# A mixture of experts behind retention: blocks of up to 768 tokens, weights loaded in slices by ScalarE, tokens transposed between products

## Chip, cores and metric

One Trainium2 chip, one core. The metric is the device time of one execution in microseconds (us). The engines are TensorE (PE; its weight loads are PEld), VectorE (DVE), ScalarE (ACT), GpSimd (POOL) and SyncE (SP). Each has its own instruction stream, and all share 16 DMA engines.

## What is computed

Retention for 8 sequences of 576 tokens with 8 heads, and then a mixture of 8 experts in which a token takes the expert of the token before it or its own best one. Every token has exactly one expert. Cut to what matters here:

```python
for b in range(B):                       # 8 x 576 tokens, D = 512
    for s in range(S):
        fresh_e = int(np.argmax(logits[b, s]))
        e = fresh_e if s == 0 or local_gate[b, s] < 0.5 else prev_e
        ...
        h = np.maximum(x[b, s] @ w1[e], 0.0)      # 512 -> 1024
        out[b, s] = p[e] * (h @ w2[e])            # 1024 -> 512
```

All of it is float32. w1 and w2 of one expert are 2 MB each.

## The kernel before, in words

**First stage** (lines 82 to 406). Retention and routing run over 36 chunks of 128 tokens. The rows x go to a DRAM buffer `xd`; `route` scatters each token's number and gate value into a DRAM table `slots` sorted by expert (L323, GpSimd, 36 scatters, each ordered behind the one before). At its end VectorE cuts each expert's tokens into blocks and writes a table `desc`: for block j the arm of the Switch, the expert, the first row, and whether it is used. The cut (L346 to L349) takes blocks of FULL = 256 tokens and leaves a last one of up to TMAX = 512.

**Expert stage** (lines 409 to 507). `step(j)` reads the arm's number for block j on every engine (L485) and jumps into one of 10 bodies, one for each width in SIZES (multiples of 32 from 256 up), or into a last one that finishes the work (L492). 17 steps are unrolled. An arm does this:

- `load(j + 1)`: SP loads the rows of `slots` (L433), GpSimd gathers the tokens into `xg` 128 at a time (L435, four gathers), SP loads the next block's w1 and w2, four transfers of 512 KB each (L444). w1 has two buffers, w2 three.
- `block(j, T)`: TensorE transposes each group of 128 tokens (L468, four transposes into one of two PSUM buffers `xgps`). A copy takes it to `xT`: even groups by VectorE (L470), odd ones by ScalarE (L472).
- TensorE then runs group 0 of the block before, which was held back for this place: `group(j - 1, 0)`, eight products 128x128 by 128x512 (L453), scaled by VectorE (L456) and scattered to `out` by GpSimd (L457).
- The first layer: for each of 8 slices m, four products of width T into `hps` (L478, three PSUM buffers), and a ReLU on ScalarE into `hT` (L480).
- The second layer for groups 1 and up of this block (L453).

A float32 product shows as two MATMUL instructions in the trace: 16 for a group of the second layer, 64 for the first layer of a block. The scheduler of the tile framework may move independent instructions inside an arm, but not across the Switch.

Of the kernel before, what the change touches and what calls it, by code (L numbers as in the profile page):

```python
# [9 lines left out]
F32 = mybir.dt.float32  # L10
BF16 = mybir.dt.bfloat16
I32 = mybir.dt.int32
Act = mybir.ActivationFunctionType
Alu = mybir.AluOpType
AX = mybir.AxisListType
ET = mybir.EngineType
# [3 lines left out]
P = 128  # L20
B, H, S, DH = 8, 8, 576, 64
D = H * DH
E, F = 8, 1024
DK, FK = D // P, F // P
# [7 lines left out]

CAP = NTOK
Q = 4
FULL = 256
TMAX = 512
GMAX = TMAX // P

NBLK = E + 1 + (NTOK - E - TMAX) // FULL
NSURE = 2 * E + 1  # L40

SIZES = [0, P, FULL] + list(range(FULL + 32, TMAX + 1, 32))
NOWHERE = 2 * NTOK
GW = 32

# [2 lines left out]
def kernel(  # L48
# [10 lines left out]
    nc = tc.nc  # L59

    def pool(stack, name, bufs, space=None):
        kw = {} if space is None else {"space": space}
        return stack.enter_context(tc.tile_pool(name=name, bufs=bufs, **kw))
# [3 lines left out]
    w1s = [keep.tile([P, FK, DK, P], F32, name="w1s0")]  # L67
    w2s = [keep.tile([P, FK, D], F32, name="w2s0")]
# [5 lines left out]
    desc = keep.tile([1, 4, NBLK + 1], I32, name="desc")  # L74
    make_identity(nc, ident)

    xgs = [keep.tile([P, GMAX, D], F32, name=f"xg{i}") for i in range(2)]
    for t in xgs:
# [3 lines left out]
    with ExitStack() as part:  # L82
# [23 lines left out]
        for k in range(DK):  # L106
# [5 lines left out]
            out=mask, in_=mask, compare_op=Alu.is_ge, fill=0.0,  # L112
# [8 lines left out]
        def number(name, shape, pattern, base=0, channel=0, dtype=F32):  # L121
# [11 lines left out]
        before = once.tile([P, P], BF16, name="before")  # L133
        nc.gpsimd.memset(before, 1.0)
        nc.gpsimd.affine_select(
            out=before, in_=before, compare_op=Alu.is_gt, fill=0.0,
# [17 lines left out]
                            in_=empty.rearrange("p r t -> p (r t)"))  # L154
# [187 lines left out]
        n = rt.tile([P, E], F32, name="n")  # L342
        nc.vector.tensor_tensor(n, base, base0, op=Alu.subtract)
        nb = rt.tile([P, E], F32, name="nb")
        nbi = rt.tile([P, E], I32, name="nbi")
        nc.vector.tensor_scalar(nb, n, -1.0, None, Alu.add)  # L346
        nc.vector.tensor_copy(nbi, nb)
        nc.vector.tensor_scalar(nbi, nbi, FULL.bit_length() - 1, None, Alu.arith_shift_right)
        nc.vector.tensor_copy(nb, nbi)  # L349
# [28 lines left out]
        nc.vector.tensor_tensor(at, one_of_blk, its_first, op=Alu.subtract)  # L378
        nc.vector.tensor_scalar(at, at, float(FULL), None, Alu.mult)
        nc.vector.tensor_tensor(its_n, its_n, at, op=Alu.subtract)  # L380
        more = rt.tile([P, (NBLK + 1)], F32, name="more")
        nc.vector.tensor_scalar(more, its_n, float(TMAX), None, Alu.is_gt)
        over = rt.tile([P, (NBLK + 1)], F32, name="over")
        nc.vector.tensor_scalar(over, its_n, -float(FULL), None, Alu.add)
        nc.vector.tensor_tensor(over, over, more, op=Alu.mult)
        sizes = rt.tile([P, (NBLK + 1)], F32, name="sizes")
        nc.vector.tensor_tensor(sizes, its_n, over, op=Alu.subtract)
        used = rt.tile([P, NBLK + 1], F32, name="used")
        nc.vector.tensor_scalar(used, sizes, 0.0, None, Alu.is_gt)
        kind = rt.tile([P, NBLK + 1], F32, name="kind")  # L390
        nc.vector.tensor_copy(kind, used)
        for t in SIZES[1:-1]:
            nc.vector.scalar_tensor_tensor(kind, sizes, float(t), kind, Alu.is_gt, Alu.add)

        ends = rt.tile([P, NBLK + 1], F32, name="ends")
        nc.vector.tensor_tensor(ends[:, 1:], used[:, 0:NBLK], used[:, 1:], op=Alu.subtract)
        nc.vector.scalar_tensor_tensor(kind[:, 1:], ends[:, 1:], float(len(SIZES)), kind[:, 1:],
                                       Alu.mult, Alu.add)
# [4 lines left out]
        nc.vector.scalar_tensor_tensor(at, its_e, float(CAP), at, Alu.mult, Alu.add)  # L403
        nc.vector.tensor_scalar(more, sizes, 0.0, float(E * CAP - TMAX), Alu.is_le, Alu.mult)
        nc.vector.tensor_tensor(at, at, more, op=Alu.max)
# [1 line left out]


    io = pool(ctx, "io", 2)
    mid = pool(ctx, "mid", 2)  # L410
    ps_x = pool(ctx, "ps_x", 2, PSUM)
    ps_h = pool(ctx, "ps_h", 3, PSUM)
    ps_y = pool(ctx, "ps_y", 3, PSUM)
    CUT = 4

    later = pool(ctx, "later", 1)
    w1s += [later.tile([P, FK, DK, P], F32, name="w1s1")]
    w2s += [later.tile([P, FK, D], F32, name=f"w2s{i}") for i in range(1, 3)]  # L420
    hTs = [later.tile([P, FK, TMAX], F32, name=f"hT{i}") for i in range(2)]
    slot_of = [later.tile([P, GMAX, 2], I32, name=f"slot{i}") for i in range(3)]

    def load(j):

        slot = slot_of[j % 3]
        e = nc.values_load(desc[0:1, 1, j:j + 1], engines=[ET.SP], min_val=0, max_val=E - 1,
                           skip_runtime_bounds_check_because="a count of experts before it")
        at = nc.values_load(desc[0:1, 2, j:j + 1], engines=[ET.SP], min_val=0, max_val=E * CAP - TMAX,
                            skip_runtime_bounds_check_because="the blocks end where the rows do")  # L430
        used = nc.values_load(desc[0:1, 3, j:j + 1], engines=[ET.SP], min_val=0, max_val=1,
                              skip_runtime_bounds_check_because="a comparison")
        nc.sync.dma_start(out=slot, in_=slots[bass.ds(at, TMAX), :].rearrange("(g p) t -> p g t", p=P))  # L433
        for g in range(GMAX):
            nc.gpsimd.indirect_dma_start(  # L435
                out=xgs[j % 2][:, g, :], out_offset=None, in_=xd,
                in_offset=bass.IndirectOffsetOnAxis(ap=slot[:, g, 0:1], axis=0),
                bounds_check=NTOK - 1, oob_is_err=False)
        f = FK // CUT
        for t, src in ((w1s[j % 2].rearrange("p m k f -> p (m k f)"), w1),  # L440
                       (w2s[j % 3].rearrange("p m d -> p (m d)"), w2)):
            for i in range(CUT):
                cols = slice(i * f * D, (i + 1) * f * D)
                nc.sync.dma_start(out=t[:, cols],  # L444
                                  in_=src[bass.ds(e, 1)].rearrange("o p x -> (o p) x")[:, cols],
                                  cond=used > 0)

    def group(j, g, M):

        hT, slot, w = hTs[j % 2], slot_of[j % 3], w2s[j % 3]  # L450
        yps = ps_y.tile([P, D], F32, name="yps")
        for m in range(FK):
            nc.tensor.matmul(yps[0:M], lhsT=hT[:, m, g * P:g * P + M], rhs=w[:, m, :],  # L453
                             start=(m == 0), stop=(m == FK - 1))
        y = io.tile([P, D], F32, name="y", bufs=4)
        nc.vector.tensor_scalar(y[0:M], yps[0:M], slot.bitcast(F32)[0:M, g, 1:2], None, Alu.mult)  # L456
        nc.gpsimd.indirect_dma_start(  # L457
            out=out, out_offset=bass.IndirectOffsetOnAxis(ap=slot[0:M, g, 0:1], axis=0),
            in_=y[0:M], in_offset=None, bounds_check=NTOK - 1, oob_is_err=False)

    def block(j, T):
        xg = xgs[j % 2]
        groups = [(g, min(P, T - g * P)) for g in range(-(-T // P))]
        xT = mid.tile([P, DK, TMAX], F32, name="xTs")
        for g, M in groups:
            xps = ps_x.tile([P, DK, P], F32, name="xgps")
            for c in range(DK):
                nc.tensor.transpose(xps[:, c, 0:M], xg[0:M, g, c * P:(c + 1) * P], ident[0:M, 0:M])  # L468
            if g % 2 == 0:
                nc.vector.tensor_copy(xT[:, :, g * P:g * P + M], xps[:, :, 0:M])  # L470
            else:
                nc.scalar.copy(xT[:, :, g * P:g * P + M], xps[:, :, 0:M])  # L472
        if j:
            group(j - 1, 0, P)
        for m in range(FK):
            hps = ps_h.tile([P, TMAX], F32, name="hps")
            for c in range(DK):
                nc.tensor.matmul(hps[:, 0:T], lhsT=w1s[j % 2][:, m, c, :], rhs=xT[:, c, 0:T],  # L478
                                 start=(c == 0), stop=(c == DK - 1))
            nc.scalar.activation(hTs[j % 2][:, m, 0:T], hps[:, 0:T], Act.Relu)  # L480
        for g, M in groups[1:]:
            group(j, g, M)

# [1 line left out]
        return nc.values_load(desc[0:1, 0, j:j + 1], min_val=0, max_val=len(SIZES),  # L485
                              skip_runtime_bounds_check_because="a count of sizes")

    load(0)

    def step(j):  # L490
        kind = kind_of(j)
        for k in tc.Switch(kind, len(SIZES) + 1):  # L492
            if k == len(SIZES):
                if j:
                    group(j - 1, 0, P)
            elif SIZES[k] and j < NBLK:
                load(j + 1)
                block(j, SIZES[k])

    for j in range(NSURE):  # L500
        step(j)

    more = nc.values_load(desc[0:1, 3, NSURE - 1:NSURE], min_val=0, max_val=1,
                          skip_runtime_bounds_check_because="a comparison")
    with tc.If(more > 0):
        for j in range(NSURE, NBLK + 1):
            step(j)
# [54 lines left out]
```

## Time and profile before

| | us |
|---|---|
| median of three runs | 992.52 (991.65 to 996.45) |
| the profiled execution: its time | 998.53 |
| its span, first to last instruction | 996.8 |
| PE busy in the span | 792.8 (80%) |
| DVE, ACT, POOL busy | 183.5, 116.9, 191.1 |
| mean granted TensorE clock, of 2.4 GHz | 0.906 |
| one fill of an `xg` buffer at the start (L79, POOL) | 1.80 |
| one copy of a transposed group by ScalarE (L472), mean | 0.57 |
| one comparison of the table of widths (L393, DVE; nine of them) | 0.19 |

The trace has lists of instructions in order of time, sums of waits by line, the sequencers' own instructions by line, and windows with the clock and the DMA rate. "Issue" as the cause of a wait means that the engine waited for nothing that the profile shows. In a timeline each row gives start, duration, engine, line, tiles, shape and count; brackets hold the idle time before it and what ended it.

### The profile page before, as it was taken

What the parts mean: (1) busy time and instruction counts of PE and PEld (TensorE: products, weight loads), DVE (VectorE), ACT (ScalarE), POOL (GpSimd) and SP (SyncE); (2) the same over time, 40 slices, a digit from 0 to 9 for tenths busy, and PEclk for the clock granted to TensorE, in tenths of its full rate; (3) what the DMA queues carried; (4) which work ended last, traced back from release to release, by engine and by line L of the source; (5) the groups of instructions that cost most, each with busy time, mean ns of one, the idle gap of its engine ahead of it and who ended that gap; (6) DMA issues with size and microseconds to landing.
All of it is one profiled execution on the core that took longest, in us unless ns stands there. A gap on an engine that the chain in (4) does not pass through costs nothing. (4 is left out here: it accounts for less than half of the span.)

```text
span 996.8 us, 12627 instructions
## 1 busy us (share of the span) xinstructions
PE 792.8 (80%) x4385; PEld 508.5 (51%) x4385; DVE 183.5 (18%) x486; ACT 116.9 (12%) x291; POOL 191.1 (19%) x208
## 2 busy tenths in 40 slices
PE   5999886868046898599959859887985986998793
PEld 5777675746034444363635536364553644546351
DVE  3565562645400001000000000100000010000000
ACT  1222221212001000010101101010110101001010
POOL 4123233222220202020220202022020121202200
PEclk9999897989568899899979979997997999898898
DMA  8787774761087206433360651336065153315000
GB/s 329 257 231 201 206 216 129 201 197 54 3 299 279 76 12 212 122 128 98 135 236 14 214 178 61 127 125 216 15 211 184 56 191 122 151 40 189 23 20 22
DMA packets 49499, 144.11 MB, mean 145 GB/s; under 512 B 16476, under 2 KB 16604, under 8 KB 44512
## 3 DMA queue, kind: packets, MB, share of 16 engines
q1 hardware_dynamic: 37776, 114.38, 34.8%
q0 software_dynamic: 9616, 23.12, 7.2%
q14 instruction: 288, 2.36, 0.8%
q8 instruction: 91, 1.49, 0.8%
q10 hardware_dynamic: 1728, 2.76, 0.7%
HBM read 129.41 MB, written 19.47 MB: 149 GB/s over the span
## 5 line engine op out<-in xcount | busy, mean ns | idle before, releaser
L453 PE MATMUL yps<-w2s,hT 128*128 128x512 f32 (+3 forms) x656 | 303.7, 619 | 1.1 <-DVE y L456 1.1
L478 PE MATMUL hps<-xTs,w1s 128*128 128x256 f32 (+4 forms) x1024 | 266.0, 422 | 23.5 <-issue 22.6
L478 PEld LDWEIGHTS hps<-xTs,w1s 128*128 128x128 f32 x1024 | 199.2, 195 | 94.2 <-issue 41.9
L453 PEld LDWEIGHTS yps<-w2s,hT 128*128 128x128 f32 (+3 forms) x656 | 121.8, 189 | 162.5 <-issue 160.2
L456 DVE TENSOR_SCALAR y<-yps,slot 128x512 f32<-128x512 f32 (+3 forms) x41 | 30.7, 749 | 497.1 <-PE yps L453 470.4
L468 PE MATMUL xgps<-ident,xg 128*128 128x128 f32 (+3 forms) x164 | 25.2, 298 | 115.9 <-DVE xTs L470 80.6
L457 POOL DMA_INDIRECT out_dram<-y,slot x41 | 40.7, 993 | 396.1 <-DVE y L456 382.2
L435 POOL DMA_INDIRECT xg<-xd,slot x68 | 68.8, 1012 | 205.9 <-issue 129.4
L480 ACT ACTIVATE hT<-hps 128x256 f32<-128x256 f32 (+4 forms) x128 | 53.3, 417 | 422.7 <-PE hps L478 358.4
L468 PEld LDWEIGHTS xgps<-ident,xg 128*128 128x128 f32 (+3 forms) x164 | 19.8, 160 | 129.9 <-DVE xTs L470 84.0
L174 PE MATMUL sps<-ld 64*128 64x128 f32 x576 | 52.8, 314 | 31.1 <-DVE sT L178 20.7
L323 POOL DMA_INDIRECT slots<-slot,posi x36 | 37.1, 1030 | 158.2 <-DMA slots<-slot,posi 94.8
L174 PEld LDWEIGHTS sps<-ld 64*128 64x128 f32 x576 | 43.0, 209 | 33.6 <-DVE sT L178 23.2
L178 DVE TENSOR_TENSOR sT<-sps,mask 128x512 f32<-128x512 f32 x72 | 46.5, 683 | 39.9 <-PE sps L174 39.8
L470 DVE COPY xTs<-xgps 128x512 f32<-128x512 f32 (+3 forms) x24 | 14.9, 619 | 176.9 <-issue 83.4
L194 PE MATMUL ops<-sT,vs 128*64 128x128 f32 x576 | 44.9, 303 | 1.8 <-POOL vs L167 1.8
L167 POOL TENSOR_TENSOR vs<-ld,deck 128x512 f32<-128x512 f32 x36 | 37.3, 1046 | 33.1 <-DMA ld<-in_qkv_dram 26.7
L215 ACT COPY state<-kv 64x256 f32<-64x256 f32 x64 | 23.4, 366 | 160.0 <-PE kv L210 159.2
L194 PEld LDWEIGHTS ops<-sT,vs 128*64 128x64 f32 x576 | 35.1, 151 | 7.7 <-issue 2.9
L200 PE MATMUL ops<-ld,state 128*128 128x128 f32 (+1 forms) x256 | 37.9, 292 | 0.0
L472 ACT COPY xTs<-xgps 128x512 f32<-128x512 f32 (+1 forms) x17 | 9.6, 566 | 226.1 <-PE xgps L468 226.1
L200 PEld LDWEIGHTS ops<-ld,state 128*128 128x128 f32 x256 | 31.9, 196 | 5.9 <-issue 5.9
(117 smaller groups left out, 297.8 us busy)
## 6 DMA issues: line engine op xcount, KB each, us to landing
ld<-in_qkv_dram SPq DMA_DIRECT2D x36, 1024.0 KB
w1s<-in_w_dram SPq DMA_DIRECT2D x68, 512.0 KB
w2s<-in_w_dram SPq DMA_DIRECT2D x68, 512.0 KB
xd<-x SPq DMA_DIRECT2D x36, 256.0 KB
decq<-in_dq_dram ACTq DMA_DIRECT2D x9, 256.0 KB
xg<-xd,slot POOLq DMA_INDIRECT x68, 4.4
out_dram<-y,slot POOLq DMA_INDIRECT x41, 2.8
slots<-slot,posi POOLq DMA_INDIRECT x36, 5.7
```

What stands on the lines that cost most here:

```text
L167: nc.gpsimd.tensor_tensor(vs.rearrange("p (h d) -> p h d", h=H), vn.rearrange("p (h d) -> p h d", h=H), deck[:, m, :].unsqueeze(2).to_broa ...
L174: nc.tensor.matmul(sps[u][:, c, :], lhsT=kT[r, c, :], rhs=qT[r, c, :], start=True, stop=True, skip_group_check=True)
L178: nc.vector.tensor_tensor(sT[:, u], sps[u], (mask2 if m == MID else mask).unsqueeze(1).to_broadcast([P, HP, P]), op=Alu.mult)
L194: nc.tensor.matmul(ops[r, c, :], lhsT=vs[:, h * DH:(h + 1) * DH], rhs=sT[:, u, c, :], start=(c == 0), stop=(m == 0), skip_group_check=True)
L200: nc.tensor.matmul(ops[:, c, 0:n], lhsT=states[(i + 1) % 2][:, c, :], rhs=qT[:, c, 0:n], start=False, stop=True, skip_group_check=True)
L323: nc.gpsimd.indirect_dma_start(out=slots, out_offset=bass.IndirectOffsetOnAxis(ap=posi[:, k:k + 1], axis=0), in_=slot[:, k, :], in_offset= ...
L435: nc.gpsimd.indirect_dma_start(out=xgs[j % 2][:, g, :], out_offset=None, in_=xd, in_offset=bass.IndirectOffsetOnAxis(ap=slot[:, g, 0:1], a ...
L453: nc.tensor.matmul(yps[0:M], lhsT=hT[:, m, g * P:g * P + M], rhs=w[:, m, :], start=(m == 0), stop=(m == FK - 1))
L457: nc.gpsimd.indirect_dma_start(out=out, out_offset=bass.IndirectOffsetOnAxis(ap=slot[0:M, g, 0:1], axis=0), in_=y[0:M], in_offset=None, bo ...
L468: nc.tensor.transpose(xps[:, c, 0:M], xg[0:M, g, c * P:(c + 1) * P], ident[0:M, 0:M])
L478: nc.tensor.matmul(hps[:, 0:T], lhsT=w1s[j % 2][:, m, c, :], rhs=xT[:, c, 0:T], start=(c == 0), stop=(c == DK - 1))
L480: nc.scalar.activation(hTs[j % 2][:, m, 0:T], hps[:, 0:T], Act.Relu)
```

## The change

Blocks: FULL becomes 512 and TMAX 768, so an expert of up to 768 tokens is one block; the steps unrolled fall from 17 to 9, and the widths (arms) rise to 18. A width above 512 is run as two halves per slice m. Weights: no longer SP but ScalarE's queue loads them, w1 and w2 of one slice m (256 KB each) behind the activations of that slice; w2 has two buffers instead of three. Tokens: the transposes of group g stand behind product g + 1 of the held-back group, all copies are ScalarE's, and `xT` has one buffer instead of two. The load of token rows moves behind them. The functions `turn`, `part` and `weights_of` are new.

```diff
-FULL = 256
-TMAX = 512
+FULL = 512
+TMAX = 768
 GMAX = TMAX // P
+TN = 512
...
-NSURE = 2 * E + 1
+NSURE = E + 1
-SIZES = [0, P, FULL] + list(range(FULL + 32, TMAX + 1, 32))
+SIZES = [0, P] + list(range(2 * P, TMAX + 1, 32))
...
-        nc.vector.tensor_scalar(nb, n, -1.0, None, Alu.add)
+        nc.vector.tensor_scalar(nb, n, float(2 * FULL - TMAX - 1), None, Alu.add)
...
-    mid = pool(ctx, "mid", 2)
+    mid = pool(ctx, "mid", 1)
...
-    w2s += [later.tile([P, FK, D], F32, name=f"w2s{i}") for i in range(1, 3)]
+    w2s += [later.tile([P, FK, D], F32, name="w2s1")]
...
-    def load(j):
+    def load_tokens(j):
...
-        for t, src in ((w1s[j % 2].rearrange("p m k f -> p (m k f)"), w1),
-                       (w2s[j % 3].rearrange("p m d -> p (m d)"), w2)):
-            for i in range(CUT):
-                cols = slice(i * f * D, (i + 1) * f * D)
-                nc.sync.dma_start(out=t[:, cols],
-                                  in_=src[bass.ds(e, 1)].rearrange("o p x -> (o p) x")[:, cols],
-                                  cond=used > 0)
...
+    def weights_of(j):
+        e = nc.values_load(desc[0:1, 1, j:j + 1], engines=[ET.Activation], min_val=0, max_val=E - 1,
...
+        used = nc.values_load(desc[0:1, 3, j:j + 1], engines=[ET.Activation], min_val=0, max_val=1,
...
+        def part(m):
+            for t, src in ((w1s[j % 2][:, m].rearrange("p k f -> p (k f)"), w1), (w2s[j % 2][:, m], w2)):
+                nc.scalar.dma_start(
+                    out=t, in_=src[bass.ds(e, 1)].rearrange("o p x -> (o p) x")[:, m * D:(m + 1) * D],
+                    cond=used > 0)
+        return part
...
+    def group(j, g, M, between=None):
+        hT, slot, w = hTs[j % 2], slot_of[j % 3], w2s[j % 2]
         for m in range(FK):
             nc.tensor.matmul(yps[0:M], lhsT=hT[:, m, g * P:g * P + M], rhs=w[:, m, :],
                              start=(m == 0), stop=(m == FK - 1))
+            if between:
+                between(m)
...
-        for g, M in groups:
+        def turn(g, M):
             xps = ps_x.tile([P, DK, P], F32, name="xgps")
             for c in range(DK):
                 nc.tensor.transpose(xps[:, c, 0:M], xg[0:M, g, c * P:(c + 1) * P], ident[0:M, 0:M])
-            if g % 2 == 0:
-                nc.vector.tensor_copy(xT[:, :, g * P:g * P + M], xps[:, :, 0:M])
-            else:
-                nc.scalar.copy(xT[:, :, g * P:g * P + M], xps[:, :, 0:M])
+            nc.scalar.copy(xT[:, :, g * P:g * P + M], xps[:, :, 0:M])
         if j:
-            group(j - 1, 0, P)
+            group(j - 1, 0, P, lambda m: turn(*groups[m - 1]) if 1 <= m <= len(groups) else None)
+        else:
+            for g in groups:
+                turn(*g)
+        load_tokens(j + 1)
+        part = weights_of(j + 1)
+        n = -(-T // TN)
         for m in range(FK):
-            hps = ps_h.tile([P, TMAX], F32, name="hps")
-            for c in range(DK):
-                nc.tensor.matmul(hps[:, 0:T], lhsT=w1s[j % 2][:, m, c, :], rhs=xT[:, c, 0:T],
-                                 start=(c == 0), stop=(c == DK - 1))
-            nc.scalar.activation(hTs[j % 2][:, m, 0:T], hps[:, 0:T], Act.Relu)
+            for i in range(n):
+                cols = slice(i * T // n, (i + 1) * T // n)
+                hps = ps_h.tile([P, TN], F32, name="hps")
+                for c in range(DK):
+                    nc.tensor.matmul(hps[:, 0:T // n], lhsT=w1s[j % 2][:, m, c, :], rhs=xT[:, c, cols],
+                                     start=(c == 0), stop=(c == DK - 1))
+                h = nc.scalar.activation(hTs[j % 2][:, m, cols], hps[:, 0:T // n], Act.Relu)
+            with tc.issue_after(h.ins):
+                part(m)
...
-    load(0)
+    load_tokens(0)
+    part = weights_of(0)
+    for m in range(FK):
+        part(m)
...
-                load(j + 1)
                 block(j, SIZES[k])
```

## Rows read from the trace of the kernel before

**Rows 1.** Timeline of TensorE, expert stage: start us, us, instructions, count [idle before].

```profile
286.98 1.09 PE L468 MATMUL xgps<-ident,xg 128*128 128x128 f32 x4 [33.36 <-DMA xg<-xd,slot]
...
290.90 15.59 PE L478 MATMUL hps<-xTs,w1s 128*128 128x256 f32 x64 [0.87 <-ACT xTs L472]
...
337.18 22.51 PE L478 MATMUL hps<-xTs,w1s 128*128 128x416 f32 x64
359.52 20.88 PE L453 MATMUL yps<-w2s,hT 128*128 128x512 f32 x48
380.33 1.10 PE L468 MATMUL xgps<-ident,xg 128*128 128x128 f32 x8
...
391.43 14.05 PE L478 MATMUL hps<-xTs,w1s 128*128 128x256 f32 x64 [3.04 <-issue]
...
423.78 0.68 PE L468 MATMUL xgps<-ident,xg 64*128 64x64 f32 x4 [10.55 <-DVE xTs L470]
...
432.69 17.39 PE L478 MATMUL hps<-xTs,w1s 128*128 128x320 f32 x64
449.92 14.04 PE L453 MATMUL yps<-w2s,hT 128*128 128x512 f32 x32
...
974.46 7.10 PE L453 MATMUL yps<-w2s,hT 128*128 128x512 f32 x16 [1.09 <-DVE y L456]
```

**Rows 2.** Waits of TensorE: who, for what, us in total, times, longest.

```profile
PE xgps L468 <- DVE xTs L470: 80.6, 8, 11.9
...
PE hps L478 <- issue: 22.6, 7, 4.3
```

**Rows 3.** Timeline of DVE and SP around two entries into an arm.

```profile
380.44 0.74 DVE L456 TENSOR_SCALAR y<-yps,slot 32x512 f32<-32x512 f32 x1 [6.23 <-PE yps L453]
...
382.67 2.50 SPq L444 DMA_DIRECT2D w1s<-in_w_dram  x4
...
390.64 0.69 DVE L470 COPY xTs<-xgps 128x512 f32<-128x512 f32 x1 [9.46 <-issue]
...
933.38 0.69 DVE L470 COPY xTs<-xgps 128x512 f32<-128x512 f32 x1 [6.22 <-issue]
```

**Rows 4.** By line: arm number read (L485), arm begun (L492); last numbers are us.

```profile
L485 DVEq TENSOR_LOAD <-desc x1: 302/302/302, 383.3 to 383.3; - x1
...
L492 DVEq BRANCH_PREFETCH_HINT  x1: 39/39/39, 390.3 to 390.3; - x1
...
L485 PEldq TENSOR_LOAD <-desc x1: 314/314/314, 373.8 to 373.8; - x1
...
L492 PEldq BRANCH_PREFETCH_HINT  x1: 40/40/40, 378.9 to 378.9; - x1
```

**Rows 5.** Windows: length, busy PE, PEld, DVE, ACT, POOL, clock, DMA share, GB/s.

```profile
382.00:398.00 16.00, 12.96 (x46) 8.29 (x45) 1.44 (x2) 1.40 (x4) 5.35 (x6) 1.00 0.88 306
...
331.50:416.00 84.50, 78.69 (x238) 41.99 (x236) 5.18 (x7) 8.37 (x18) 11.99 (x12) 1.00 0.27 88
```

**Rows 6.** Groups by line: ScalarE's ReLU; SP's issues of w1 (ns min/median/max).

```profile
L480 ACT ACTIVATE hT<-hps 128x256 f32<-128x256 f32 (+4 forms) x128 | 53.3, 417 | 422.7 <-PE hps L478 358.4 <-DMA xg<-xd,slot 42.0 <-DMA w2s<-in_w_dram 22.2
...
L444 SPq DMA_DIRECT2D w1s<-in_w_dram x68: 73/333/1477, 278.2 to 930.2; - x68
```

**Rows 7.** Timeline at the change of stages: SP's load of slots, GpSimd's second gather.

```profile
276.75 0.42 SPq L433 DMA_DIRECT2D slot<-slots  x1
...
281.45 1.00 POOL L435 DMA_INDIRECT xg<-xd,slot  x1 [0.31 <-issue]
```

**Rows 8.** Landing times by line: L323 262 to 277, 100 to 220; L435 279 to 300, 935 to 942.

```profile
DMA to landing us min/median/max: 3.6/3.6/3.9
...
DMA to landing us min/median/max: 4.1/6.5/9.6
...
DMA to landing us min/median/max: 6.5/7.0/7.5
...
DMA to landing us min/median/max: 2.1/2.2/3.0
```

More of the change, by code (lines that the diff above doesn't have):

```diff
@@ L413 @@
     ps_y = pool(ctx, "ps_y", 3, PSUM)
-    CUT = 4
     later = pool(ctx, "later", 1)
     w1s += [later.tile([P, FK, DK, P], F32, name="w1s1")]
-    w2s += [later.tile([P, FK, D], F32, name=f"w2s{i}") for i in range(1, 3)]
+    w2s += [later.tile([P, FK, D], F32, name="w2s1")]
     hTs = [later.tile([P, FK, TMAX], F32, name=f"hT{i}") for i in range(2)]
     slot_of = [later.tile([P, GMAX, 2], I32, name=f"slot{i}") for i in range(3)]
-    def load(j):
+    def load_tokens(j):
         slot = slot_of[j % 3]
-        e = nc.values_load(desc[0:1, 1, j:j + 1], engines=[ET.SP], min_val=0, max_val=E - 1,
-                           skip_runtime_bounds_check_because="a count of experts before it")
         at = nc.values_load(desc[0:1, 2, j:j + 1], engines=[ET.SP], min_val=0, max_val=E * CAP - TMAX,
                             skip_runtime_bounds_check_because="the blocks end where the rows do")
-        used = nc.values_load(desc[0:1, 3, j:j + 1], engines=[ET.SP], min_val=0, max_val=1,
-                              skip_runtime_bounds_check_because="a comparison")
         nc.sync.dma_start(out=slot, in_=slots[bass.ds(at, TMAX), :].rearrange("(g p) t -> p g t", p=P))
@@ L438, in load @@
                 bounds_check=NTOK - 1, oob_is_err=False)
-        f = FK // CUT
-        for t, src in ((w1s[j % 2].rearrange("p m k f -> p (m k f)"), w1),
-                       (w2s[j % 3].rearrange("p m d -> p (m d)"), w2)):
-            for i in range(CUT):
-                cols = slice(i * f * D, (i + 1) * f * D)
-                nc.sync.dma_start(out=t[:, cols],
-                                  in_=src[bass.ds(e, 1)].rearrange("o p x -> (o p) x")[:, cols],
-                                  cond=used > 0)
-    def group(j, g, M):
-        hT, slot, w = hTs[j % 2], slot_of[j % 3], w2s[j % 3]
+    def weights_of(j):
+        e = nc.values_load(desc[0:1, 1, j:j + 1], engines=[ET.Activation], min_val=0, max_val=E - 1,
+                           skip_runtime_bounds_check_because="a count of experts before it")
+        used = nc.values_load(desc[0:1, 3, j:j + 1], engines=[ET.Activation], min_val=0, max_val=1,
+                              skip_runtime_bounds_check_because="a comparison")
+        def part(m):
[6 more added lines that the diff above has]
+        hT, slot, w = hTs[j % 2], slot_of[j % 3], w2s[j % 2]
         yps = ps_y.tile([P, D], F32, name="yps")
```

## The prediction, made before the changed kernel ran

> **What bounds the kernel now.** I read the timeline of TensorE first. The expert stage runs from the first product of the first layer at 290.90 us to the last product, which starts at 974.46 and lasts 7.10, so it ends at 981.56 [rows 1]: 690.7 us. Inside a block the products follow each other without a gap. A full group of the second layer takes (380.33 - 359.52) / 3 = 6.94 us, and a first layer of width 320 takes 449.92 - 432.69 = 17.23 us for 64 instructions, 0.00084 us per column of each. The sixteen widths read off the timeline (the first and the widest stand in [rows 1]) are eight times 256 and 416, 320, 352, 320, 352, 288, 352, 288, together 4736 columns. So the work is 41 groups x 6.94 = 284.5, first layers 4736 x 64 x 0.00084 = 254.6, and 39 transposed groups (two come before the stage) at 1.10 / 2 = 0.55, so 21.5: 560.6 us. The other 130.1 us are not work.
>
> The waits of TensorE say where they are: 80.6 us in 8 waits of the transposes for VectorE's copy and 22.6 us in 7 waits before a first layer [rows 2]. One of each kind, in turn, closes every pair of blocks: 3.04 us at 391.43 and 10.55 us at 423.78 [rows 1]. Two waits for y (of about 1.1 us each, one in [rows 1]) make 2.1. The remaining 24.8 us I put down to the clock: products after such a gap run partly at 1.2 GHz (the first layer of width 256 took 15.59 us after a wait and 14.05 elsewhere [rows 1]).
>
> Why is VectorE's copy late? The reader should look at its last y of the arm before (380.44) and its copy (390.64): 9.46 us idle, for no event that the profile shows [rows 3]. The sequencers' rows fill it: VectorE reads the arm's number at 383.3 and begins the arm at 390.3, 7.0 us later. TensorE read its number at 373.8 and began at 378.9, while its queued products ran to 380.4, so its entry is hidden [rows 4]. VectorE cannot start earlier, since its last instruction of an arm is the last y. Its entry also coincides with SP's weights (four of the eight transfers from 382.67 [rows 3]), which move 306 GB/s in that stretch [rows 5]. At the last block there are no weights to load, and the same wait is 6.22 us [rows 3].
>
> **The change, part by part.** The sum is made against the profiled execution (span 996.8, time 998.53); the median is 992.52, 6.0 lower, and I take the difference off the median.
>
> Wider blocks: the pairs above become single blocks of 672, 576, 608, 576, 608, 544, 608 and 544, none over 768. Columns (4736), groups (41) and weight loads of TensorE stay the same: two halves per slice repeat what the two blocks did. Work stays at 284.5 + 254.6 and 35 groups transposed inside the stage, 19.3: 558.4.
>
> Copies by ScalarE: VectorE's entry now stands before y of the held-back group only. TensorE reaches that point after eight products and five transposed groups, 6.94 + 5 x 0.55 = 9.7 us; VectorE needs about 2.1 (383.3 less the end of y at 381.18) and 7.0 at the most. And nothing needs that y at once, as there are three PSUM buffers. ScalarE enters its arm behind its last ReLU, while TensorE still has four groups (27.8 us) to do. A copy of 0.57 us hides behind a turn and a product, 0.55 + 0.87; the last one hides behind the last products. So the 80.6 and 22.6 us go, and with them most of the slow clock. If that cover were gone, a turn would cost another copy, 0.6 us x 35 = 21 us.
>
> What is late next: at each of eight entries the first product of the held-back group needs a PSUM buffer that VectorE frees, and across the Switch it seems to wait for the last y of the arm, as at 974.46, where it waited 1.09 us although its buffer's own reader was long done [rows 1]. Before, transposes stood there. 8 x 1.09 = 8.7 us; the other end of the bound is 0.
>
> Weights on ScalarE's queue: 16 issues per block. SP's took 0.33 us each, at the longest 1.48 [rows 6], and 2.50 / 4 = 0.63 with their register work [rows 3]. Per slice m ScalarE then does two ReLUs of 0.42 [rows 6] and two issues, 2.1 us, against TensorE's 254.6 / 64 = 4.0. I cost it at nothing, hidden behind the first layer; at 1.48 + 0.30 an issue it would be 4.4 us, 0.4 too long per slice, 26 us over 64 slices. Bytes: 33.5 MB instead of 67, 4.2 MB in some 70 us, 60 GB/s against the 306 that were moved [rows 5]. They land before the groups of the second layer end, so arms are entered with quiet DMA queues. Issues past SP: the slot load waits for nothing new there.
>
> The start: ScalarE can load block 0 as soon as the table is ready, about 264 us, while SP did so only behind its slot load at 276.75 [rows 7]. The last three scatters, which that slot load waits for, then meet about 12 us of weights. Their landing takes 3.6 us now and 6.5 where DMA was busy earlier [rows 8]. Two of them lengthened make 2 x 2.9 = +5.8 us; the bounds are 0 and 3 x (9.6 - 3.6) = 18. The gathers gain: 2.2 instead of 7.0 us, -4.8 [rows 8]. The first transposes move from 286.98 to 288.0. Six groups must come, 1.31 us apart [rows 7], so 6.6 more, then a transpose at the low clock (1.09) and a copy (0.6): the first layer starts at 296.3 instead of 290.9.
>
> Small edits: eight more comparisons of widths (0.19 each) on shorter tables run while the scatters still hold the slot load; the larger fill of xg (half as much again, 2 x 0.9 us) lies behind the first loads of the first stage. Nothing for each; at worst 3 us together.
>
> **Sum.** 296.3 + 558.4 + 8.7 + 1.5 (cold start, 15.59 - 14.05) = 864.9 for the last product's end, and 15.2 us of tail as now: span 880.1, 116.7 less than 996.8. 992.5 - 116.7 = 875.8, say **876 us**.
>
> **Will the clock hold?** From 331.5 to 416 it was 1.00, with TensorE busy 78.7 of 84.5 us [rows 5]. The stage would now be some 560 us without such gaps, longer than any stretch seen; I assume 2.4 GHz.
>
> **Rivals.**
> (a) TensorE's own entry shows. Its number was read 6.6 us before its products ended and the entry took 5.1 [rows 4], so only 1.5 us are spare. If ScalarE's transfers were still under way there, the entry would take VectorE's 7.0 plus 2.1: 2.5 us exposed, and with 1.5 of low clock 4.0 x 8 = 32: 908 us. Against it: 27.8 us of groups lie between the last slice and the entry. The Trainium skill (Runtime: NRT & Kernel Launch, Instruction fetch mechanics) says that a taken branch out of the window already fetched stops the engine until a DMA has brought the target. The trace agrees: 5.1 us in a quiet stretch, 7.0 beside weights [rows 4].
> (b) ScalarE becomes the bound in the first layer, priced above: 902 us. For it: issues of 1.48 us exist; against: the typical one is 0.33 [rows 6].
> (c) Slower than before. The slices land one by one: each issue on ScalarE waits until the one before has landed. A block's first layer is 254.6 / 8 = 31.8 us and its ReLUs 16 x 0.42 = 6.7; the 116.7 us saved are 14.6 per block. So it decides from (31.8 + 14.6 - 6.7) / 16 = 2.5 us per slice. At 0.63 + 4 us (between the quiet and the busy landing of a gather [rows 8]) the layer takes 80.8, 49.0 more x 8 = 392: 1268 us. Against it: SP's issues followed 0.63 us apart [rows 3], with no wait for a landing. The Trainium skill (DMA: Bandwidth & Descriptors, Anatomy of one DMA) gives 2.0 us fixed per transfer, so an estimate of 2.6 us for 256 KB; by that price the layer would take 48.3 and the kernel 1008 us. No run here shows slices of that size.
> (d) The change does not do what it says: an expert above 768 tokens would still take two blocks. The widths exclude it.
>
> **How the numbers follow.** Forecast 0.75, (a) 0.10, (b) 0.08, (c) 0.03; 0.04 for something better still. The forecast's own range is 862 (no wait for y, start as now) to 890 (18 us at the start). With (a) and (b) the range is 862 to 908. About 0.5% can be told from no change. Faster takes everything but (c) and a hundredth: 0.96, same 0.01, slower 0.03.
>
> **What would show it.** Right: no idle before L468; a wait of about 1 us before the first L453 of an arm, eight times; 1024 and 656 products as before; a clock of 1.00 from 300 us on; ScalarE's issues 0.6 us apart between activations; scatters after 264 us landing in over 6 us. Wrong: gaps of TensorE inside the first layer that end with ScalarE (b, c), or at the entries with "issue" (a), or a clock under 1.00 without a gap before it.

## The result, and the profile after

The changed kernel takes 867.51 us (median of four runs, 865.79 to 872.71) against 992.09 for the kernel before (988.17 to 996.45): a ratio of 0.8752, 95% interval 0.8699 to 0.8806. The prediction was 876, range 862 to 908.

First the page of the changed kernel: the span, busy times, the granted clock in 40 slices, the bytes, and the groups that answer to [rows 2, 3, 6].

```profile
span 864.6 us, 11666 instructions
...
PE 765.9 (89%) x4385; PEld 494.6 (57%) x4385; DVE 170.6 (20%) x470; ACT 129.6 (15%) x315; POOL 177.6 (21%) x194
...
PEclk9999999999955799999999999999999999999998
...
HBM read 92.17 MB, written 19.47 MB: 129 GB/s over the span
...
L454 PE MATMUL yps<-w2s,hT 128*128 128x512 f32 (+3 forms) x656 | 291.7, 594 | 8.8 <-issue 7.7
L489 PE MATMUL hps<-xTs,w1s 128*128 128x304 f32 (+3 forms) x1024 | 258.2, 414 | 0.0
...
L491 ACT ACTIVATE hT<-hps 128x304 f32<-128x304 f32 (+3 forms) x128 | 53.3, 417 | 215.5 <-PE hps L489 213.0
```

As many product instructions as before (656 and 1024), no idle time ahead of any first-layer product, 8.8 us ahead of the second layer's, and once the stage has begun no slice with a low clock until the last. The kernel before read 129.41 MB: the halved weight loads are 33.6 of the 37.2 MB between them, and the gathers of tokens, 54 instead of 68, the rest.

The timeline of TensorE, to be read against [rows 1]:

```profile
246.09 0.25 PE L305 MATMUL seen<-one,ones 128*128 128x32 bf16 x4
281.57 3.04 PE L472 MATMUL xgps<-ident,xg 128*128 128x128 f32 x12 [35.24 <-DMA xg<-xd,slot]
...
287.39 1.33 PE L489 MATMUL hps<-xTs,w1s 128*128 128x336 f32 x2
...
325.75 34.61 PE L454 MATMUL yps<-w2s,hT 128*128 128x512 f32 x80
361.46 1.95 PE L454 MATMUL yps<-w2s,hT 128*128 128x512 f32 x4 [1.09 <-issue]
363.25 0.60 PE L472 MATMUL xgps<-ident,xg 128*128 128x128 f32 x4
363.68 1.02 PE L454 MATMUL yps<-w2s,hT 128*128 128x512 f32 x2
364.55 0.60 PE L472 MATMUL xgps<-ident,xg 128*128 128x128 f32 x4
...
365.84 0.60 PE L472 MATMUL xgps<-ident,xg 128*128 128x128 f32 x4
...
846.31 7.11 PE L454 MATMUL yps<-w2s,hT 128*128 128x512 f32 x16 [1.09 <-DVE y L459]
```

At the entry near 361 us only 1.09 us is idle; then transposes and products alternate without a gap. The sum of TensorE's waits shows that the other entries look the same, and that [rows 2]'s 80.6 and 22.6 us are gone:

```profile
PE yps L454 <- issue: 7.7, 7, 1.1
PE yps L454 <- DVE y L459: 1.1, 1, 1.1
```

The expert stage, from the first first-layer product to the end of the last product, was 690.7 us before; it is 846.31 + 7.11 - 287.39 = 566.0 now. Windows over it, before and after (length, busy PE, PEld, DVE, ACT, POOL, granted clock, DMA share, GB/s). In the kernel before, and below it over one entry of VectorE, the leaving of the old arm and then the way into the new one:

```profile
290.90:981.50 690.60, 585.20 (x1836) 339.22 (x1836) 44.12 (x63) 62.36 (x144) 104.54 (x104) 0.93 0.38 129
...
380.40:383.20 2.80, 2.80 (x14) 1.78 (x14) 0.74 (x1) 0.58 (x1) 0.89 (x1) 1.00 0.16 16
383.90:390.20 6.30, 4.49 (x11) 1.71 (x9) 0.00 (x0) 0.00 (x0) 0.00 (x0) 1.00 0.96 313
```

The same three windows in the changed kernel:

```profile
287.00:853.00 566.00, 557.24 (x1827) 325.39 (x1825) 29.96 (x40) 73.29 (x165) 85.64 (x86) 1.00 0.28 85
...
360.40:363.20 2.80, 1.74 (x4) 0.82 (x5) 0.74 (x1) 0.00 (x0) 0.89 (x1) 1.00 0.06 15
363.90:366.70 2.80, 2.80 (x13) 1.54 (x12) 0.00 (x0) 1.39 (x3) 0.00 (x0) 1.00 0.03 9
```

Idle TensorE in the stage fell from 690.6 - 585.2 = 105.4 to 8.8 us, and its busy time by 28.0, most of that slow clock after the gaps (0.93 became 1.00). Together that is 124.6 us of the 132.2 by which the two profiled spans differ (996.8 and 864.6); the rest is a first stage 7.3 us shorter, a way from there to the first layer 3.8 longer and a tail 4.0 shorter. That the medians differ by 124.6 us as well is chance: the profiled execution of the kernel before (998.53) stands 6.4 us above its median, that of the changed kernel (866.36) 1.2 below. An entry of VectorE became shorter too: its way into the arm is 6.3 us where the DMA engines are 96% busy and 2.8 where they are 3% busy. The sequencers' rows, as in [rows 4], number read and arm begun:

```profile
L498 PEldq TENSOR_LOAD <-desc x1: 317/317/317, 353.7 to 353.7; - x1
L498 DVEq TENSOR_LOAD <-desc x1: 316/316/316, 363.3 to 363.3; - x1
...
L508 PEldq BRANCH_PREFETCH_HINT  x1: 45/45/45, 358.9 to 358.9; - x1
L508 DVEq BRANCH_PREFETCH_HINT  x1: 51/51/51, 366.7 to 366.7; - x1
```

VectorE begins its arm at 366.7 and nothing needs it there: its first work, a y, comes at 371.10 when the held-back group's products end. TensorE's entry is 5.2 us and over at 358.9, before its queued products end at 360.36.

### The profile page after: what moved, and what is told of

It is laid out like the page before. It is cut to its first block, busy times and chain, and to the rows that moved or that the text cites. A ratio compares the mean times of both kernels' runs of the same rounds, so it can differ in the third digit from the quotient of the medians.

```text
span 864.6 us, 11666 instructions
## 1 busy us (share of the span) xinstructions
PE 765.9 (89%) x4385; PEld 494.6 (57%) x4385; DVE 170.6 (20%) x470; ACT 129.6 (15%) x315; POOL 177.6 (21%) x194
## 5 line engine op out<-in xcount | busy, mean ns | idle before, releaser
L454 PE MATMUL yps<-w2s,hT 128*128 128x512 f32 (+3 forms) x656 | 291.7, 594 | 8.8 <-issue 7.7
L489 PE MATMUL hps<-xTs,w1s 128*128 128x304 f32 (+3 forms) x1024 | 258.2, 414 | 0.0
L489 PEld LDWEIGHTS hps<-xTs,w1s 128*128 128x128 f32 x1024 | 195.1, 191 | 63.2 <-issue 4.0
L454 PEld LDWEIGHTS yps<-w2s,hT 128*128 128x128 f32 (+3 forms) x656 | 114.0, 180 | 156.7 <-issue 155.5
L491 ACT ACTIVATE hT<-hps 128x304 f32<-128x304 f32 (+3 forms) x128 | 53.3, 417 | 215.5 <-PE hps L489 213.0
L324 POOL DMA_INDIRECT slots<-slot,posi x36 | 36.9, 1024 | 155.7 <-DMA slots<-slot,posi 89.3
L429 POOL DMA_INDIRECT xg<-xd,slot x54 | 54.4, 1008 | 63.4 <-PE xgps L472 43.3
L473 ACT COPY xTs<-xgps 128x512 f32<-128x512 f32 (+3 forms) x41 | 22.3, 544 | 286.2 <-PE xgps L472 286.1
L175 PE MATMUL sps<-ld 64*128 64x128 f32 x576 | 49.9, 304 | 15.9 <-DMA ld<-in_qkv_dram 9.9
L472 PE MATMUL xgps<-ident,xg 128*128 128x128 f32 (+3 forms) x164 | 25.9, 286 | 36.1 <-DMA xg<-xd,slot 35.2
L472 PEld LDWEIGHTS xgps<-ident,xg 128*128 128x128 f32 (+3 forms) x164 | 20.8, 152 | 57.6 <-DMA xg<-xd,slot 35.3
L175 PEld LDWEIGHTS sps<-ld 64*128 64x128 f32 x576 | 40.3, 201 | 18.4 <-DVE sT L179 8.6
L216 ACT COPY state<-kv 64x256 f32<-64x256 f32 x64 | 23.4, 366 | 151.2 <-PE kv L211 150.4
L195 PEld LDWEIGHTS ops<-sT,vs 128*64 128x64 f32 x576 | 34.7, 149 | 16.1 <-POOL vs L168 11.2
L168 POOL TENSOR_TENSOR vs<-ld,deck 128x512 f32<-128x512 f32 x36 | 37.2, 1044 | 31.4 <-DMA ld<-in_qkv_dram 24.8
L218 DVE TENSOR_TENSOR xT<-ops,decq 128x512 f32<-128x512 f32 x36 | 24.6, 683 | 21.7 <-PE ops L201 20.8
```

Of the source, the lines that this page charges most:

```text
L168: nc.gpsimd.tensor_tensor(vs.rearrange("p (h d) -> p h d", h=H), vn.rearrange("p (h d) -> p h d", h=H), deck[:, m, :].unsqueeze(2).to_broa ...
L175: nc.tensor.matmul(sps[u][:, c, :], lhsT=kT[r, c, :], rhs=qT[r, c, :], start=True, stop=True, skip_group_check=True)
L195: nc.tensor.matmul(ops[r, c, :], lhsT=vs[:, h * DH:(h + 1) * DH], rhs=sT[:, u, c, :], start=(c == 0), stop=(m == 0), skip_group_check=True)
L324: nc.gpsimd.indirect_dma_start(out=slots, out_offset=bass.IndirectOffsetOnAxis(ap=posi[:, k:k + 1], axis=0), in_=slot[:, k, :], in_offset= ...
L429: nc.gpsimd.indirect_dma_start(out=xgs[j % 2][:, g, :], out_offset=None, in_=xd, in_offset=bass.IndirectOffsetOnAxis(ap=slot[:, g, 0:1], a ...
L489: nc.tensor.matmul(hps[:, 0:T // n], lhsT=w1s[j % 2][:, m, c, :], rhs=xT[:, c, cols], start=(c == 0), stop=(c == DK - 1))
```

## The experiments

Three causes were open: that the gain is the removed wait for VectorE's late entry (theory A, the prediction's); that TensorE's own entry matters, halved in number by the width (theory D); or that it is the number of blocks and their weights, bytes and queue (theory B). In all experiments conditions stand in place of the Switch, with this input's widths written in. They therefore leave out the arms for other widths and the unused blocks; the numbers hold for this input only, and no variant under the Switch itself ran. In all but f1_before_inline a long body that is never taken lies in the way, so that the engines must jump over it. Times are medians of four runs, ratios against the kernel before in the same session (998.14 us for the first four kernels, 996.2 for the last four).

**x1_before_if**: the kernel before with two nested conditions per block, as a stand-in for the Switch: one far jump in, one far jump out.

```diff
+    WIDTHS = [256, 416, 256, 320, 256, 352, 256, 320, 256, 352, 256, 288, 256, 352, 256, 288]
+    def work_of(j):
+        if j == len(WIDTHS):
+            group(j - 1, 0, P)
+        else:
+            load(j + 1)
+            block(j, WIDTHS[j])
+    def other_arms(j):
...
-        for k in tc.Switch(kind, len(SIZES) + 1):
...
+        with tc.If(kind < 1) as cmp:
+            other_arms(j)
+        with cmp.Else():
+            with tc.If(kind > 1) as inner:
+                work_of(j)
+            with inner.Else():
+                other_arms(j)
...
-    for j in range(NSURE):
+    for j in range(len(WIDTHS) + 1):
```

> Control: the kernel before, with the Switch replaced by two nested conditions per block. The one arm that this input takes stands between two long arms that it never takes (three other widths and 600 small instructions on VectorE, ScalarE and GpSimd), so every engine jumps far into the arm and far out of it, as under the Switch; the arms for all other widths and the unused blocks are left out. Theory A (VectorE's late entry into the arm holds TensorE) and theory B (the number of blocks and the bytes of their weights cost the time) both expect the time of before, 960 to 1000 us, with 60 us or more of waits of the transposes for VectorE's copy.

988.18 us, ratio 0.9878 (0.9816 to 0.994). By its time a good copy of the kernel before; by its waits it is not one. TensorE's waits:

```profile
PE xgps L468 <- issue: 74.4, 17, 6.7
...
PE xgps L468 <- DVE xTs L470: 17.0, 7, 4.3
```

Most idle time is now "issue" of TensorE itself. Its branches by line, out of the arm (the second of L514) and into the next (L511), in ns:

```profile
L511 PEldq COMPARE_BRANCH  x1: 4680/4680/4680, 374.7 to 374.7; - x1
...
L514 PEldq COMPARE_BRANCH  x2: 80/2998/5916, 368.3 to 379.4; - x2
```

5.92 + 4.68 = 10.6 us, more than the 6.6 us by which TensorE's sequencer is ahead of its products [rows 4]. So this control failed as a copy, but it shows rival (a)'s mechanism: two far jumps of TensorE don't hide. The trace of the kernel before shows where the copy differs. Its branches of the Switch, at the same entry, out of the old arm at 373.4 and into the new one at 374.4:

```profile
L558 PEldq COMPARE_BRANCH  x2: 320/2338/4356, 373.4 to 374.4; - x2
```

Under the Switch TensorE's branch out of an arm takes 0.31 to 0.43 us, behind every block of both kernels, where x1's jump out takes 3.6 to 6.3. So the Switch costs TensorE one jump, and x1 costs it two. (The other engines need 2.4 us or more from that branch to the next number, VectorE 2.8 here; why TensorE doesn't is open.)

**x2_before_if_scalare**: the same with all copies by ScalarE.

```diff
-            if g % 2 == 0:
-                nc.vector.tensor_copy(xT[:, :, g * P:g * P + M], xps[:, :, 0:M])
-            else:
-                nc.scalar.copy(xT[:, :, g * P:g * P + M], xps[:, :, 0:M])
+            nc.scalar.copy(xT[:, :, g * P:g * P + M], xps[:, :, 0:M])
```

> The control of the kernel before (two nested conditions) with one more edit: ScalarE copies every transposed group, VectorE none. Blocks stay at 256 and up to 512 tokens, weights stay with SP. Theory A: the waits of the transposes (80.6 us in the trace of before) and of the first layers (22.6) go, and most of the 24.8 us of low clock with them; with some 5 us of new short waits 115 to 125 us less than the control: 870 us, 855 to 890. Theory B: nothing that costs is touched, within 10 us of the control. Theory C (copies and width bring about half each): 60 us less, about 930.

968.16 us, ratio 0.9694 (0.9642 to 0.9746): 20 us less than x1, where theory A asked for about 870. TensorE's waits are 75.5 us "issue", and none for a copy by VectorE: the 17.0 us that had been VectorE's went, TensorE's own jumps stayed. The miss is the control's; y1 and y2 below repeat the pair without the jump out.

**f1_before_inline**: the kernel before with one condition per block and its arm in line, so that no engine jumps. Copies, blocks of 256 to 512 and SP's weights stay as before.

```diff
-        for k in tc.Switch(kind, len(SIZES) + 1):
...
+        with tc.If(kind > 0):
+            work_of(j)
```

> The kernel before with the Switch replaced by one condition per block whose arm follows in line, so that no engine jumps; VectorE still copies the even groups, blocks and weights are as before; the arms for all other widths and the unused blocks are left out. Theory A: VectorE's first copy of an arm comes 1 to 2 us after its last y, not 9.5; about 1.6 us of wait stay in eight arms, and the low clock goes: 992 - 128 + 13 = 877 us, 862 to 900. Theory B: within 10 us of the kernel before, 980 or more.

867.79 us, ratio 0.8679 (0.8608 to 0.875): the changed kernel's time with none of its parts (its ratio was 0.8752, in another session). VectorE's timeline at the place of [rows 3]'s 9.46 us:

```profile
365.36 0.74 DVE L456 TENSOR_SCALAR y<-yps,slot 32x512 f32<-32x512 f32 x1 [6.23 <-PE yps L453]
366.29 0.69 DVE L470 COPY xTs<-xgps 128x512 f32<-128x512 f32 x1 [0.19 <-DVE y L456]
```

The copy follows the last y after 0.19 us, and the stage has 568.00 - 559.25 = 8.8 us of idle TensorE at a clock of 1.00:

```profile
290.00:858.00 568.00, 559.25 (x1836) 328.08 (x1836) 44.15 (x63) 62.37 (x144) 104.51 (x104) 1.00 0.46 152
```

It still reads 129.41 MB and moves 152 GB/s in the stage, against 85 in the changed kernel. So the bytes and the queue of the weights don't set the time, and the lost time was that of the jumps.

**x3_after_if**: the changed kernel with x1's two conditions per block, which it now has 8 times instead of 16 between blocks; the edit is x1's.

> Control: the changed kernel with the Switch replaced by two nested conditions per block, as in the control of the kernel before (far jumps into the arm and out of it; other widths and unused blocks left out). Both theories: the time of the changed kernel, 867 us, 855 to 880, and the wait of about 1.1 us before the first product of an arm stays, since the arm is still one of several.

881.83 us, ratio 0.8828 (0.8776 to 0.8881), a little above the expected band. TensorE waits 8.5 us in 6 waits that the profile puts down to y, and 7.1 in 4 for "issue"; the stage is 576.5 us. TensorE's branches at the second entry:

```profile
L526 PEldq COMPARE_BRANCH  x1: 4492/4492/4492, 439.1 to 439.1; - x1
...
L529 PEldq COMPARE_BRANCH  x2: 80/1810/3541, 435.1 to 443.6; - x2
```

The jump in ends at 439.1 + 4.5 = 443.6, and the next product starts at 443.87 after 1.75 us, while the y that the wait is put down to was done at 442.15 + 0.74 = 442.89. So this wait too is TensorE's own jump. Out and in take 3.54 + 4.49 = 8.0 us here against x1's 10.6, and there are 8 such entries instead of 16: 15.6 us of waits instead of x1's 95.4.

**y1_before_onejump**: the kernel before with one far jump per block, over the never-taken body; the arm's end falls through.

```diff
+        with tc.If(kind < 1) as cmp:
+            other_arms(j)
+        with cmp.Else():
+            work_of(j)
```

> Second control: the kernel before with one condition per block and a long arm that is never taken in front of the one that is, so that every engine makes one far jump, into the arm, and falls out of it in line. TensorE's jump (4.7 us in the first control) is shorter than the 6.6 us by which it runs ahead, so it stays hidden, and VectorE's (3.4 to 6.4 us) comes after its last y as under the Switch. Theory A (VectorE's late entry into the arm holds TensorE): the third turn of the eight wide arms waits 4 to 7 us for VectorE's copy and some narrow arms 1 us before the first layer, with low clock 45 to 75 us more than the 868 of the inline kernel: 905 to 945 us. Theory D (only TensorE's own jump costs): 868 to 880 us.

911.13 us, ratio 0.9154 (0.9107 to 0.9201), inside theory A's band and far from the rival's. TensorE's waits, and the stage:

```profile
PE xgps L468 <- DVE xTs L470: 29.1, 7, 4.9
...
PE xgps L468 <- issue: 4.5, 1, 4.5
```

```profile
288.50:900.60 612.10, 577.62 (x1836) 335.40 (x1836) 44.13 (x63) 62.50 (x144) 104.56 (x104) 0.96 0.44 142
```

TensorE's single jump shows once (4.5 us). VectorE's shows seven times, about 4 us each, where the Switch cost [rows 2]'s 10 each with two jumps.

**y2_onejump_scalare**: y1 with x2's edit, all copies by ScalarE.

> The second control with one more edit: ScalarE copies every transposed group, VectorE none. Blocks of 256 and up to 512 tokens and weights by SP stay. Theory A: the waits for VectorE's copy go: 868 us, 860 to 882, without wider blocks, slices or turns between products. Theory D: the same time as the second control. Theory B (the number of blocks and their bytes cost the time): within 10 us of the second control.

862.59 us, ratio 0.867 (0.8622 to 0.8718): 48.5 us less than y1, by the change of the copying engine alone. The stage:

```profile
283.00:852.00 569.00, 562.94 (x1836) 329.08 (x1836) 29.95 (x40) 73.05 (x167) 104.58 (x104) 0.99 0.48 154
```

Against y1 idle time falls from 34.5 to 6.1 and busy time from 577.6 to 562.9, by 14.7: the clock goes from 0.96 to 0.99, so in this pair every 2 us of waiting had gone with another 1 us of slow products (in the kernel before it was 105.4 us with 24.6).

**y3_wide_two_ahead**: the changed kernel with one far jump, and two groups transposed ahead of the held-back group, so that something stands before the wait for y.

```diff
-            group(j - 1, 0, P, lambda m: turn(*groups[m - 1]) if 1 <= m <= len(groups) else None)
+            for g in groups[:2]:
+                turn(*g)
+            group(j - 1, 0, P, lambda m: turn(*groups[m + 1]) if 1 <= m <= len(groups) - 2 else None)
```

> The changed kernel with one far jump per block, as in the second control, and one edit towards a faster version: the first two groups are transposed ahead of the held-back group's first product, the others between its later products. Theory A with the reading that the 1.1 us before an arm's first product is a wait for the last y of the arm before, which two transposed groups cover: 7 x 1.1 us less than the changed kernel, 858 us, 852 to 866, and no idle time before L454 at the entries. Rival (the wait is the PSUM buffer's or the jump's own): the idle time moves ahead of the first transposes, 867 us or more.

858.93 us, ratio 0.8639 (0.8579 to 0.8698). The stage is busy from end to end:

```profile
297.40:852.10 554.70, 554.70 (x1825) 324.94 (x1824) 29.96 (x40) 72.59 (x165) 85.59 (x86) 1.00 0.28 86
```

But y4 has no wait for y either, without the two groups ahead, so the edit isn't what removed it. The row of the waits that TensorE's sequencer executes for L454 around an entry tells what did. In the changed kernel (durations in ns):

```profile
L454 PEldq EVENT_SEMAPHORE  x13: 51/51/1417, 359.0 to 361.9; - x13
...
L454 PEldq EVENT_SEMAPHORE  x1: 1417/1417/1417, 359.8 to 359.8; - x1
...
360.40 0.74 DVE L459 TENSOR_SCALAR y<-yps,slot 32x512 f32<-32x512 f32 x1 [6.24 <-PE yps L454]
```

and in y4:

```profile
L454 PEldq EVENT_SEMAPHORE  x1: 51/51/51, 366.9 to 366.9; - x1
```

Behind the Switch the first product of an arm passes a row of waits, one of them 1.42 us long; behind the condition there is one short wait. The long one begins at 359.8 and ends at 361.2, just behind the end of the old arm's last y (360.40 + 0.74 = 361.14): it fits the wait for y that the prediction named. In y4 the first product passes its wait at 366.9, before its old arm's last y begins at 370.02. So the wait belongs to the Switch's arms, not to the order of the products.

**y4_wide_shared_copies**: the changed kernel with one far jump and VectorE's copies back (x2's edit reversed).

> The changed kernel with one far jump per block and the copies shared again: VectorE the even groups, ScalarE the odd ones. Blocks of up to 768, the slices and the turns between products stay. Theory A: the third turn stands 5.5 us behind the arm's first product and VectorE, whose jump finds quiet DMA queues (3.4 us), has copied the first turn after 5 to 6 us: waits of at most 0.5 us in seven arms, 867 to 873 us. So width and interleaving hide VectorE's entry by themselves. Rival (ScalarE's copies are what the change lives on): 4 us and more in each of seven arms, 895 us or more.

861.57 us, ratio 0.8638 (0.8585 to 0.869): lower than expected, and far from the rival's figure. VectorE's first copy of a block is late by its jump and nothing waits:

```profile
370.02 0.74 DVE L459 TENSOR_SCALAR y<-yps,slot 32x512 f32<-32x512 f32 x1 [6.23 <-PE yps L454]
373.38 0.69 DVE L474 COPY xTs<-xgps 128x512 f32<-128x512 f32 x1 [2.62 <-issue]
```

The products between the transposes cover 2.62 us, and the stage has no idle time (556.3 us, clock 1.00). It is a narrow cover: the copy ends at 374.07, and the third turn, which takes the same PSUM buffer as the first, starts at 374.33. The Switch's entry is longer (366.7 less the end of y at 361.14, 5.6 us); with VectorE's copies it was not run. By the changed kernel's rows, as an estimate, it would not be covered: a copy behind 366.7 ends at 367.4 or later, and the third turn stood at 365.84, so 1.6 us or more in each of seven arms. What y4 shows is therefore that the rest of the change covers one short jump, not that ScalarE's copies are needless under the Switch.

All kernels side by side, from the timelines and windows: the end of the untouched first stage is taken as the last product into `seen`.

| kernel | last `seen` | first layer starts | from one to the other | stage | TensorE idle in it | clock |
|---|---|---|---|---|---|---|
| before | 253.4 | 290.9 | 37.5 | 690.7 | 105.4 | 0.93 |
| after | 246.1 | 287.4 | 41.3 | 566.0 | 8.8 | 1.00 |
| x1_before_if | 250.7 | 286.4 | 35.7 | 694.2 | 95.4 | 0.91 |
| x2_before_if_scalare | 255.4 | 289.5 | 34.2 | 670.6 | 77.5 | 0.93 |
| f1_before_inline | 254.6 | 290.0 | 35.4 | 568.2 | 8.8 | 1.00 |
| x3_after_if | 253.0 | 296.2 | 43.1 | 576.5 | 15.7 | 0.99 |
| y1_before_onejump | 251.3 | 288.5 | 37.2 | 612.1 | 34.5 | 0.96 |
| y2_onejump_scalare | 246.4 | 282.9 | 36.5 | 569.0 | 6.1 | 0.99 |
| y3_wide_two_ahead | 255.9 | 297.4 | 41.5 | 554.8 | 0.0 | 1.00 |
| y4_wide_shared_copies | 255.5 | 297.3 | 41.8 | 556.3 | 0.0 | 1.00 |

## Why the prediction was right, point by point

The predicted span was 880.1, the profiled one 864.6. The 15.5 us are the first stage (-7.3), the start (-1.6), the stage (-2.6) and the tail (-4.0). So the mechanism and its size in the stage were right. The medians lie closer, 867.5 measured against 876, partly by chance: the 6.0 us that the prediction took off for its profiled execution happen to offset most of the 7.3 of the first stage.

- **What was lost.** Right, and shown: without jumps (f1), or with the copies alone moved (y2 against y1), the idle time and the slow clock go. The split into waits and 24.8 us of slow clock is borne out: TensorE was busy 585.2 us for 560.6 of work, 24.6 more. The two rows that the prediction named for the slow clock don't show it, though: 15.59 us is the stage's first layer, behind 33 us without work, and the 14.05 stands behind a wait too, of 3.04 us. What shows it is the stretch around the wait of 10.55 us that ended at 423.78:

```profile
416.90:427.10 10.20, 3.32 (x7) 1.67 (x8) 1.12 (x2) 0.00 (x0) 1.14 (x2) 0.50 0.99 356
```

  The granted clock was 0.50 there, the lower level, and the group behind the wait took 8.43 us instead of 7.0. Twelve such stretches, 102.0 us, lie in the stage, and TensorE was busy in 51.6 of them; half of that, 25.8 us, is an estimate of what the lower level cost.
- **Wider blocks, copies, turns.** No idle time is left before L472 at the entries, as said. The parts don't add up, though: the copies alone (y2), the width and turns with shared copies (y4), and no jump at all (f1) each come to about the same time. They are covers of the same entry, once it is a single jump or none. Under the Switch itself, where VectorE's entry is two jumps long, they were not taken apart.
- **The wait for y.** 8 x 1.09 = 8.7 predicted, 7.7 + 1.1 = 8.8 measured. y3 and y4 place it with the Switch's arms.
- **Work.** 558.4 and 1.5 of cold start predicted, 557.2 of busy time measured. A turn adds 363.68 - 363.25 = 0.43 us in the new order, not the 0.55 of two turns back to back; 35 x 0.12 = 4.2, of which 2.7 shows.
- **Weights on ScalarE.** Costed at nothing, and nothing it was. Around one slice:

```profile
312.39 0.45 ACT L491 ACTIVATE hT<-hps 128x336 f32<-128x336 f32 x1 [1.81 <-PE hps L489]
312.69 0.34 ACTq L443 DMA_DIRECT2D w1s<-in_w_dram  x1
313.35 1.21 ACTq L443 DMA_DIRECT2D w2s<-in_w_dram  x1
314.65 0.45 ACT L491 ACTIVATE hT<-hps 128x336 f32<-128x336 f32 x1 [1.81 <-PE hps L489]
```

  The 1.81 us in the bracket are idle time of the engine, in which its sequencer issues: the issue of 1.21 us ends at 314.56, 0.09 before the next ReLU. So there was little to spare. Once it was not enough: behind an issue of 1.13 us at 527.16 the next ReLU came at 528.34, 2.14 us after the one before instead of 1.94. TensorE, with three buffers of `hps`, still waited 0.0 us ahead of L489: rival (b) is out, though by less than the prediction's typical issue of 0.33 us suggests. The issues follow 0.66 us apart and wait for no landing: rival (c) is out. The kernel before had shown as much for transfers of 256 KB, although the prediction found none: ScalarE issued nine for `decq` (L100) in 9.85 us, 1.1 us each. The Trainium skill (DMA: Bandwidth & Descriptors, Anatomy of one DMA) gives 2.0 us fixed per transfer, in a section on those that GpSimd issues; no row here shows that part for ScalarE's slices, and if it is so long, it lies beside the next transfers.
- **Rival (a).** Not here: the entry of 5.2 us ended 1.5 us before the products did. x1 and x2 show that the mechanism is real once two jumps come to 10.6 us.
- **The start.** From the last `seen` to the first layer the prediction said 5.4 more; the profiled execution has 41.3 - 37.5 = 3.8, and the four wide kernels average 41.9 against 36.1 for the six narrow ones, 5.8. In the profiled execution the last four scatters landed in

```profile
DMA to landing us min/median/max: 3.1/4.8/6.9
```

  (five scatters, one of them before the weights began), so that the slot load came 27.3 us after the last `seen` (273.35) and not 23.4: +3.9, not +5.8; and the first transposes came 8.2 us after the slot load instead of 10.2: -2.0, not -4.8. From there to the first layer it is 287.39 - 281.57 = 5.8 us, where the prediction had 8.3: the later gathers had landed by then, and three groups were turned in one go (281.57, 12 instructions).
- **Mis-sized terms.** The start was taken as a time from the span's beginning, as if the first stage were of fixed length. It is not: its end lies between 246.1 and 255.9 us in the ten profiled executions, and no relation to the width or the copies is seen. That is 7.3 of the 15.5 us. The tail was 11.2 us instead of "15.2 as now"; it was not taken apart.

## What to carry to other kernels

The engine that finishes an arm last also enters the next one last; give the first work of a data-dependent arm to engines that left the old one early, or put products between so that nothing is due within the entry (here 3 to 9 us). Several covers of one wait don't add: count what idle time is left (8.8 us here) before a further one is built. A control has to match the original in its waits and not only in its time, as x1 did not; and where an untouched stage varies by 10 us, kernels are compared by the stage that was changed.

## What the runs showed of the hardware that was not expected

- A jump's price depends on what the DMA engines do: VectorE's way into an arm took 6.3 us at 96% DMA share (313 GB/s) and 2.8 us at 3%. The other entries bear it out. In the kernel before, fourteen of VectorE's ways in met DMA engines 86 to 98% busy and took 5.6 to 7.5 us; its last two, at 4 and 6%, took 3.0 and 3.4, and the eight between blocks of the changed kernel, at 4 to 6%, 2.8 to 3.4. It is not the whole price: three first entries don't fit (VectorE's in the kernel before, 4.8 us at 8%; ScalarE's and GpSimd's in the changed kernel, 2.9 and 2.8 us at 89 and 83%). The prediction saw the two together [rows 4, 5] and took no gain from parting them: the slices, spread over the first layer, shorten VectorE's entry itself, though it was hidden by then. The profile also has two DMA queues of the kind "instruction": they moved 3.85 MB in the kernel before, 2.28 in the changed one and 0.79 in f1. The Trainium skill (Runtime: NRT & Kernel Launch, Instruction fetch mechanics) says that a taken branch out of the fetched window waits for a DMA of its target; both prices and the bytes of these queues fit that, and f1's 0.19 us fits an arm entered without a taken branch.
- TensorE hides one jump of its own (4.7 us in y1, 5.2 us with the number's reading in the changed kernel) behind queued products, and not two (10.6 us in x1). The Switch costs it only one: its branch out of an arm takes 0.31 to 0.43 us.
- The first product behind a Switch goes through a row of semaphore waits, 13 for this line around one entry, and the longest was 1.42 us; behind a plain condition it was one of 0.05 us. This is how the program was built, not a speed of the engine.
